# Strassen's scheme a second time, over two pairs of batches, in a fused attention and token-mixing kernel

## The chip, the cores and the metric

The kernel runs on one core of one Trainium2 chip. The metric is the device time of one execution in microseconds (us). A core has five engines that run side by side, each through its own instructions in order: TensorE (PE in the profile; its weight loads are PEld), VectorE (DVE), ScalarE (ACT), GpSimd (POOL) and SyncE (SP). PE writes its results to PSUM; the working memory SBUF has 128 partitions. DMAs are issued from queues: here SP loads inputs and stores results, and POOL issues DMAs that add their data to what stands at the target ("accumulating DMAs").

## What is computed

Four batches, four heads, 1088 positions, 32 features per head; float32 arithmetic to float32 accuracy.

```python
phi(x)  = outer product of S1 x and S2 x           # 8 * 8 features
kv, z   = sum over positions of phi(k) v, of phi(k)
x       = (phi(q) kv) / (phi(q) z + 1e-6)          # (4, 1088, 128): heads side by side
theta   = x @ w_theta
zr, zi  = x * cos(theta), x * sin(theta)
y       = w_tok_r @ zr + w_tok_i @ zi              # over the 1088 positions, for each batch
u       = x + y
out     = u + max(u @ w_ch, 0)
```

The two token-mixing matrices (1088 x 1088, in float64, unpacked to float32 by the kernel) make up most of the matmul work.

## The kernel before

**One order written out by hand.** The kernel first collects all its work as numbered operations: `op(engine, duration, function, writes, reads)` at lines 146 to 198. `SEQUENCE` (line 46) is a list of the 1024 numbers, and `issue` (line 206) issues the operations in that order; each engine executes its own in that order. `PLACES` gives each buffer its slot in a class of buffers (lines 277 to 286): `big` for rows of the matrices and for x, `zs` for z and raw rows, `hf`, `g3`, `g1`, `sm` for smaller things, `ps` for the eight PSUM banks.

**Attention, batch by batch.** Sums over k squared give the scale of a rounding of k to a coarse level `kb` (line 651) and a rest `r = k - kb` (line 656, VectorE). For batches 1 to 3 the product of rest and (k + level) is needed: k is loaded from memory a second time to `kh` (line 649) and the level is added to it by an accumulating DMA (line 658, through `join`, line 323). Chains of small operations (`chain`, line 777) follow, then `levels`, `den`, `numerators` and `theta_stage` (lines 968 to 1133) for each batch: PE, ACT and DVE take turns, with a cosine and a sine on ACT (lines 1048, 1050). Their result is `zt[b]`, the weights for token mixing: real chunks 0 to 7, imaginary chunks 8 to 15, and the 64 last positions of both in one tail chunk.

**Rows.** `weight` (line 581) brings the 17 rows of the matrices in: one load of 1088 KB each, two or three ACT operations, a shift on DVE and an integer addition, on DVE (line 601) or, for rows in `ROWS_ADD`, by an accumulating DMA (line 599).

**Token mixing.** Each matrix is cut at output position 544, which gives four quarters `a11` (real, first half), `a12` (imaginary, first), `a21`, `a22` (second half; line 1216). For a pair of batches (p, q), [[a11, a12], [a21, a22]] times the real and imaginary z of both is a 2 x 2 block product and is made by seven products instead of eight, in the manner of Strassen. A product (`product`, line 1239) is eight chunks of 128 positions into 544 columns, in two PSUM banks of 288 and 256 columns: 16 matmuls. The sums of z that it needs are made on DVE (`zsum`, `ztwo`), the sums of quarters (`asum`, line 1228) in place by eight accumulating DMAs ("D") or on DVE ("V"). `add` (line 1256) adds a product to x; batch q is held scaled by a power of two against p (`balance`, line 1146; `even[5]` takes it back). `finish` (line 1269) makes two or three output parts of a half: the channel matmul, its rectified sum on DVE, a transpose on DVE and four stores, or for parts of 128 columns a form without transpose and one store. `ends` adds the tail chunk.

Pairs are (0, 1) and (2, 3). Product 1 and 2 of a pair need only batch p (`early_products`, line 1302); product 1 is saved to SBUF and added to three places by accumulating DMAs (`carried`, line 1324). `pair_a` (7, 6, 4) and `pair_a_late` (5, 3) belong to the first pair, `pair_b` (6, 4, 7, 5, 3) to the second. PE runs products of the first pair between the theta stages of batches 2 and 3.

Of the kernel before, what the change touches and what calls it, by code (L numbers as in the profile page):

```python
# [37 lines left out]
KDMA = (False, True, True, True)  # L38
RDMA = (False,) * 4
QDMA = (False,) * 4  # L40
ROWS_ADD = (3, 5, 7, 9, 10, 11, 12, 13, 14, 15, 16)
SUMS = {"30": "D", "20": "D", "10": "V", "40": "D", "32": "V"}
CARRY = {(0, 1): "dma", (2, 3): "dma"}
# [203 lines left out]
def kernel(  # L247
# [1144 lines left out]
    def pair_b(pair):  # L1392
# [24 lines left out]
        for j in BOTH:  # L1417
            ends(s5, q, 1, (j,))
# [94 lines left out]
```

## Time and profile before

| | |
|---|---|
| time, three runs | 229.39 us median (228.37 to 229.68) |
| the profiled execution, its own time | 229.23 us |
| its span in the profile | 227.4 us |
| granted PE clock, mean | 0.992 |
| DMA from SP's queue | 30.30 MB, 39.0% of the 16 engines' span |
| DMA from POOL's queue | 16.26 MB, 37.3% |

Busy times are shares of the span. A matmul of float32 leaves two weight loads and two matmul records in the trace. A line number is that of the helper that recorded an operation: 331 for a matmul, 311 and 318 for VectorE's two-input operations, 325 for an accumulating DMA; so the tiles tell more than the line (`ps<-big,zs` is a token-mixing matmul: rows and z into PSUM).

### The profile page before, as it was taken

To read this page: it belongs to the slowest core of one execution; us is meant where nothing else is said; L and a number is where in the kernel's file an instruction comes from. 1 tells how busy PE (TensorE), PEld (TensorE's weight loads), DVE (VectorE), ACT (ScalarE), POOL (GpSimd) and SP (SyncE) were. 2 spreads that over 40 slices of the span, in tenths; PEclk is the share of its full clock that TensorE was granted. 3 is DMA by queue.
4 is the path that set the end of the run, shared out by engine and by line. 5 is a ranking of instruction groups with operands and counts; after the bars stand their busy time and mean duration, and the time that the engine had idled before them with its cause. 6 is when DMAs were issued, how large, how long until landed. Compare 5 with 4: busy or idle time off the path is not lost.

```text
span 227.4 us, 4055 instructions
## 1 busy us (share of the span) xinstructions
PE 217.8 (96%) x1486; PEld 182.2 (80%) x1486; DVE 171.0 (75%) x388; ACT 126.1 (55%) x260; POOL 55.2 (24%) x92
## 2 busy tenths in 40 slices
PE   7999999998979999899989999999999999999993
PEld 3898999976867886588868788888888888888882
DVE  2799999999999989789997917985483663504763
ACT  2988798999999997999997545730000000000000
POOL 1067960001116300013322361968000000000000
PEclk9999999999979999999999999999999999999999
DMA  4999999994999999299999899999973000331442
GB/s 130 421 420 312 383 353 417 419 425 147 246 299 188 299 257 273 89 291 242 275 243 207 255 191 167 176 191 194 198 128 52 0 0 3 62 58 23 69 74 58
DMA packets 28888, 46.80 MB, mean 206 GB/s; under 512 B 18757, under 2 KB 19013, under 8 KB 26693
## 3 DMA queue, kind: packets, MB, share of 16 engines
q1 hardware_dynamic: 22532, 30.30, 39.0%
q0 software_dynamic: 6336, 16.26, 37.3%
q8 instruction: 11, 0.18, 0.3%
q14 instruction: 9, 0.07, 0.1%
HBM read 28.07 MB, written 2.23 MB: 133 GB/s over the span
## 4 chain that ended last, share of the span: by engine, by line
PE 54%; DVE 24%; DMA 10%; ACT 7%; issue 3%; POOL 0%; SPq 0%; DVEq 0%; ACTq 0%; POOLq 0%
PE ps L331 49%; DMA big<-big 5%; DVE big L311 5%; DMA zs<-w_tok 4%; DVE g L311 3%; DVE sm L318 2%; PE ps L366 2%; DVE hf L315 2%; DVE big L315 2%; DVE sm L311 2%; ACT big L591 2%; PE ps L1035 1%; DVE sm L315 1%; DVE lv L311 1%; PE ps L1087 1%
## 5 line engine op out<-in xcount | busy, mean ns | idle before, releaser
L331 PE MATMUL ps<-big,zs 128*128 128x288 f32 (+2 forms) x498 | 116.2, 387 | 2.2 <-DVE zs L311 1.4
L331 PEld LDWEIGHTS ps<-big,zs 128*128 128x128 f32 x498 | 91.2, 191 | 20.5 <-DVE zs L311 1.5
L325 POOL DMA_DIRECT2D big<-big x35 | 33.5, 1347 | 89.9 <-DVE big L315 29.7
L591 ACT ACTIVATE big<-zs 128x544 f32<-128x544 f32 (+1 forms) x33 | 23.3, 727 | 0.7 <-DMA zs<-w_tok 0.7
L594 ACT ACTIVATE big<-zs 128x1088 int32<-128x1088 uint32 (+1 forms) x18 | 21.4, 1190 | 3.1 <-DMA big<-big 1.7
L318 DVE SCALAR_TENSOR_TENSOR big<-ps,even,big 128x288 f32<-128x288 f32 (+2 forms) x23 | 10.5, 483 | 16.1 <-PE ps L331 15.8
L331 PE MATMUL ps<-mf,big 128*128 128x96 f32 x72 | 14.5, 295 | 0.1
L311 DVE TENSOR_TENSOR zs<-ps,g 128x768 f32<-128x768 f32 (+2 forms) x20 | 12.5, 630 | 2.1 <-ACT g L1050 1.7
L315 DVE TENSOR_SCALAR big<-big 128x1088 int32<-128x1088 int32 x17 | 12.2, 725 | 1.3 <-ACT big L591 1.1
L331 PEld LDWEIGHTS <-hf 128*128 128x128 f16 (+1 forms) x144 | 11.9, 105 | 1.2 <-issue 0.8
L311 DVE TENSOR_TENSOR big<-big,ps 128x288 f32<-128x288 f32 (+1 forms) x12 | 5.1, 433 | 9.9 <-PE ps L331 9.8
L311 DVE TENSOR_TENSOR g<-lv 128x768 f32<-128x768 f32 x12 | 11.2, 952 | 1.4 <-PE ps L1087 1.2
L331 PE MATMUL ps<-w,big 128*128 128x128 f32 (+1 forms) x76 | 12.2, 299 | 0.0
L331 PEld LDWEIGHTS ps<-w,big 128*128 128x128 f32 x76 | 10.7, 202 | 1.8 <-PE ps L331 0.6
L318 DVE SCALAR_TENSOR_TENSOR big<-ps,big 128x288 f32<-128x288 f32 (+1 forms) x15 | 6.5, 434 | 6.6 <-PE ps L331 6.5
L331 PEld LDWEIGHTS ps<-mf,big 128*128 128x128 f32 x72 | 10.9, 191 | 0.4 <-issue 0.4
L311 DVE TENSOR_TENSOR big<-big,hf 128x1152 f32<-128x1152 f32 x8 | 11.0, 1385 | 0.0
L325 POOL DMA_DIRECT2D big<-hf x9 | 10.3, 1300 | 2.8 <-DVE sm L315 2.0
L331 PE MATMUL ps<-mv,hf 128*128 128x96 f16 x108 | 10.8, 206 | 0.1
L331 PE MATMUL ps<-big,big 128*128 128x128 f32 x72 | 10.9, 279 | 0.0
L331 PE MATMUL ps<-sbk,g 128*128 128x64 f32 x72 | 9.5, 272 | 0.0
L331 PEld LDWEIGHTS ps<-big,big 128*128 128x128 f32 x72 | 9.3, 192 | 0.1
(195 smaller groups left out, 381.0 us busy)
## 6 DMA issues: line engine op xcount, KB each, us to landing
zs<-w_tok SPq DMA_DIRECT2D x17, 1088.0 KB, 9.6
big<-big POOLq DMA_DIRECT2D x24, 272.0 KB, 8.7
big<-big POOLq DMA_DIRECT2D x11, 544.0 KB, 9.1
big<-k_l SPq DMA_DIRECT2D x7, 576.0 KB, 7.6
big<-q_l SPq DMA_DIRECT2D x4, 576.0 KB, 6.6
big<-v_l SPq DMA_DIRECT2D x4, 576.0 KB, 9.1
big<-hf POOLq DMA_DIRECT2D x3, 576.0 KB, 10.1
big<-hf POOLq DMA_DIRECT2D x6, 272.0 KB, 10.9
```

The costliest lines, as they stand in the source:

```text
L311: eng.tensor_tensor(out=o, in0=a, in1=b, op=f)
L315: (eng or V).tensor_scalar(out=o, in0=a, scalar1=s1, scalar2=s2, op0=op0, **kw)
L318: (eng or V).scalar_tensor_tensor(out=o, in0=a, scalar=s, in1=b, op0=op0, op1=op1)
L325: op("G", n * 2.55e-3, lambda: G.dma_start(dst(), src(), accum_op=ALU.add), w, r, kind=2)
L331: T.matmul(o, lhs, rhs, start=start, stop=stop, skip_group_check=True)
L366: T.matmul(nowhere() if out is None else out, idle()[:, 0:P], idle(), start=True, stop=True, skip_group_check=True)
L591: op("A", 0.19 + (c1 - c0) * 0.0009, lambda c0=c0, c1=c1, scale=scale, alpha=alpha: A.activation(dfn()[:, c0:c1], words_of(raw(), n)[1][:, ...
L594: op("A", 0.22 + n * 0.0009, lambda: A.activation(stp(), words_of(raw(), n)[0].bitcast(U32), AF.Copy, scale=2.0**-29), [stp], [raw])
L1035: T.transpose(x()[:, i], xs()[:, off + i * P:off + (i + 1) * P], ident())
L1087: T.transpose(tr()[:, i * P:(i + 1) * P], qp()[:, i * H + 2 * n:i * H + 2 * n + 2].rearrange("p h i j -> p (h i j)"), ident())
```

## The change

Products 4, 5 and 3 of both pairs use the same quarter (a22, a11, a12) with the z of two pairs. `joint` makes each of them for both pairs at once as a 2 x 2 block product: the quarter is cut into two halves of its chunks and two halves of 272 columns, the two z into their halves of chunks, and seven block products of four chunks and 272 columns take the place of eight (Winograd's form). The sums of blocks of the quarter are `blocks`: two of four on GpSimd, two on VectorE, four operations of 272 columns each; the sums of z are four operations of 512 columns on VectorE. Two of the block products are copied to SBUF by ACT and added to x by accumulating DMAs (`spill`), the others by VectorE (`land`).

So that the batches of both pairs can be used together, batch 2 too is now balanced against batch 0, which puts three scalings on ACT and a ratio on VectorE ahead of its theta stage. The rest goes with it or stands by itself: products 1, 6 and 7 are collected in SBUF (`keep`, `more`) and spread from there by accumulating DMAs; the sum for a11 becomes a negation on ACT and an accumulating DMA ("N"); k plus level is made on VectorE from the k that is there (`KDMA` "V"), without the second load; rows 1, 2, 4, 6 and 8 join `ROWS_ADD`; the sine that loads ACT's table is the first thing on ACT; several small operations are grouped; `SEQUENCE` (968 numbers), `PLACES` and `FILLS` are new.

```diff
-KDMA = (False, True, True, True)
+KDMA = (False, 'V', 'V', 'V')
-ROWS_ADD = (3, 5, 7, 9, 10, 11, 12, 13, 14, 15, 16)
-SUMS = {"30": "D", "20": "D", "10": "V", "40": "D", "32": "V"}
-CARRY = {(0, 1): "dma", (2, 3): "dma"}
+ROWS_ADD = (3, 5, 6, 7, 8, 9, 10, 11, 12, 13, 14, 15, 16, 2, 4, 1)
+SUMS = {"30": "D", "20": "D", "10": "N", "40": "D", "32": "V"}
+JOINT = ("4", "5", "3")
+BLOCKS = {"4": "GGVV", "5": "GGVV", "3": "GGVV"}
+QT = 272
...
+        if eng == "A":
+            pred.update(self.leader)
+            self.leader = self.leader or [o.i]
...
-    op("V", 1.5, constants, [hm, bdm, halfpi, ups, ones, grids], [])
-    op("A", 0.3, lambda: A.activation(warm(), halfpi(), AF.Sin), [warm], [halfpi])
+    op("V", 0.1, lambda: V.memset(halfpi(), math.pi / 2.0), [halfpi], [])
+    op("V", 1.5, constants, [hm, bdm, ups, ones, grids], [])
+    op("A", 1.5, lambda: A.activation(warm(), halfpi(), AF.Sin), [warm], [halfpi])
...
-        if KDMA[b]:
+        if KDMA[b] and KDMA[b] != "V":
             at("loadh", b)
...
-        if KDMA[b]:
+        if KDMA[b] == "V":
+            vop(n, lambda: tt(V, flat(kh()), kc(), flat(kb()), ALU.add), [kh], [kx, kb], lk=1)
+        elif KDMA[b]:
             join(n, lambda: flat(kh()), lambda: flat(kb()), [kh], [kb])
...
-            ts(e[:, 0:2], e[:, 0:2], TINY * TINY, ALU.max, 1.0 / (TINY * TINY), ALU.min)
+            ts(e[:, 0:2], squares()[:, 0:b + 1:b], TINY * TINY, ALU.max, 1.0 / (TINY * TINY), ALU.min)
...
-            if how == "D":
+            if how == "N":
+                op("A", act(HT), lambda i=i: A.mul(dst.ap(i), dst.ap(i), -1.0), [dst.key(i)], [])
+            if how in "DN":
                 join(HT, lambda i=i: dst.ap(i), lambda i=i: y.ap(i), [dst.key(i)], [y.key(i)])
...
+    def keep(name, to):
+        u = buf("hf", (HT,), F32, name)
+        at("acc", name)
+        for j, (c0, c1) in enumerate(PARTS):
+            op("A", act(c1 - c0), lambda j=j, c0=c0, c1=c1: A.copy(u()[:, c0:c1], to.out(j)), [(u, j)], [to.parts[j]])
+        return u
+
+    def more(name, u, to):
+        at("acc", name)
+        for j, (c0, c1) in enumerate(PARTS):
+            vop(c1 - c0, lambda j=j, c0=c0, c1=c1: tt(V, u()[:, c0:c1], u()[:, c0:c1], to.out(j), ALU.add), [(u, j)],
+                [to.parts[j]])
+
+    def spread(b, h, u, c0=0, n=HT, w=None):
+        at("carry", b, "_", h)
+        y = w or u
+        if b and not w:
+            y = buf("hf", (n,), F32, "uq")
+            op("A", act(n), lambda: A.mul(y(), u(), evens[b]()[:, 5:6]), [y], [u, evens[b]])
+        c0 += h * HT
+        join(n, lambda: xT[b]()[:, c0:c0 + n], lambda: y()[:, :n], cells(xT[b], c0, c0 + n), [y])
...
+    def joint(n, a, im, mine, targets, cls, last=False):
...
+        X1, X2 = fresh(x1), fresh(x2)
+        E, F = slab("s" + n, cls)
+        how = BLOCKS[n]
+
+        def zs(k_, d, x, y):
+            at("zj", n, k_)
+            vop(NB * P, lambda: tt(V, d[1](), x[1](), y[1](), ALU.subtract), d[2](), x[2]() + y[2](), lk=1)
+
+        def blocks(k_, d, x, y, f):
+            at("aj", n, k_)
+            eng = how[k_]
+            for i in range(NB):
+                op(eng, pool_(QT) if eng == "G" else dve(QT), lambda i=i: tt(
+                    G if eng == "G" else V, d[0](i), x[0](i), y[0](i), f), [d[1](i)], [x[1](i), y[1](i)], lk=1)
+
+        lo, hi = (0, QT), (QT, HT)
+
+        def sub(k_, to, z, x, cuts=None):
+            at("j", n, k_)
+            for c0, c1 in cuts or [(0, QT)]:
+                to.add((0,), NB * ((c1 - c0) * 4 / 2400 + 0.005), [lambda j, i=i, c0=c0, c1=c1: (
+                    to.out(0)[:, c0:c1], z[0](i), x[0](i)[:, c0:c1]) for i in range(NB)],
+                    z[2]() + [x[1](i) for i in range(NB)])
+            to.close()
...
+        zs(1, X1, z2t, z0t)
+        blocks(0, E, tr, br, ALU.add)
+        zs(2, X2, z2b, X1)
+        blocks(1, F, E, tl, ALU.subtract)
+        zs(3, z2t, z2b, z2t)
+        blocks(2, tr, tl, tr, ALU.subtract)
+        Z, Y, W = [Sum(f"j{n}{c}", (lo,)) for c in "ZYW"]
+        sub(1, Z, z0t, tl)
+        spill(1, Z, bb0, both, lo)
+        sub(2, Y, z0b, bl)
+        blocks(3, bl, bl, F, ALU.subtract)
+        zs(4, z0b, z0b, X2)
...
+        land("y", Y, bb0, lo)
+        sub(6, Z, X2, F)
+        spill(2, Z, bb2, both, lo)
+        sub(5, W, X1, E)
+        land("w", W, bb2, hi, False)
+        sub(7, Z, z2t, tr)
+        land("z", Z, bb2, hi, False)
+        sub(4, Z, z0b, br)
+        land("q", Z, bb0, hi)
...
+        sub(3, W, z2b, bl)
+        land("v", W, bb2, lo)
+        for b in (bb0, bb2):
+            for h in both:
+                if n != "5" or h:
+                    done(b, h, LAST if last and b == bb2 else PARTS)
...
-            largest(pair, j)
-            theta_stage(b, xT[b] if j == 0 else balance(pair))
+            largest(b)
+            theta_stage(b, balance(b) if b else xT[b])
...
+    (pa, qa), (pb, qb) = PAIRS
+    for n in JOINT:
+        if n == "4":
+            joint("4", a22, 1, (pa, pb), ([(1, True)], (pa, pb)), "g3")
+        elif n == "5":
+            joint("5", a11, 0, (pa, pb), ([(0, False), (1, True)], (qa, qb)), "zs")
+        else:
+            joint("3", a12, 1, (qa, qb), ([(0, True)], (qa, qb)), "g3", True)
```

More of the change, by code (lines that the diff above doesn't have):

```diff
@@ L1158, in ratio @@
             stt(e[:, 5:6], e[:, 1:2], 0.5, e[:, 2:3], ALU.mult, ALU.mult)
[L1160 removed]
+        op("V", 1.0, ratio, [even], [(squares, 0), (squares, b)], lk=6)
         return even
@@ L1237, in asum, with product @@
                    [x.key(i), y.key(i)], lk=1)
-    def product(name, to, zz, aa, joint=True, tail=None):
+    def product(name, to, zz, aa, joint=True, tail=None, step=2):
         each = tuple(range(len(to.cuts)))
@@ L1254, in ends, with add @@
             [(zt[b], NG), (rows[NK - 1], h)])
-    def add(name, pair, b, h, to):
-        even = evens[pair]
-        for j, cut in enumerate(to.cuts):
+    def add(name, b, h, to, cuts=None):
+        for j, cut in enumerate(cuts or to.cuts):
             at("acc", name, "_", j)
@@ L1348, in ztwo, with zneg, parts_of, product4 @@
                                                         ALU.subtract), [dst[1](g)], [x[1](g), y[1](g)], lk=1)
+    def zneg(name, dst, x, y):
+        at("zc", name)
+        for g in range(NG):
+            c0, c1 = g * GC, min(g * GC + GC, NF)
+            vop((c1 - c0) * P, lambda c0=c0, c1=c1: stt(dst[0](c0, c1), x[0](c0, c1), -1.0, y[0](c0, c1), ALU.mult,
+                                                        ALU.subtract), [dst[1](g)], [x[1](g), y[1](g)], lk=1)
+    def parts_of(pair):
+        p, q = pair
+        return part(zt[p], 0), part(zt[p], 1), part(zt[q], 0), part(zt[q], 1)
+    def product4(pair):
+        p, q = pair
+        s4 = Sum(f"p4{p}")
+        product(f"4{p}", s4, part(zt[p], 1), a22, tail=(p, 1))
+        add(f"4{p}", p, 1, s4)
+        done(p, 1)
+    def product5(pair, joint):
+        p, q = pair
+        x = str(p)
+        s5 = Sum("p5" + x)
+        product("5" + x, s5, part(zt[p], 0), a11, joint)
+        add("5" + x, q, 0, s5)
+        at("m", "e" + x)
+        for js in [BOTH] if joint else [(j,) for j in BOTH]:
+            ends(s5, q, 1, js)
+        s5.close()
+        add("5" + x + "h", q, 1, s5)
+        done(q, 1)
+    def product3(pair, cuts):
+        p, q = pair
+        s3 = Sum(f"p3{p}", cuts)
+        product(f"3{p}", s3, part(zt[q], 1), a12, cuts is PARTS, tail=(q, 0))
+        add(f"3{p}", q, 0, s3)
+        done(q, 0, cuts)
     def pair_a(pair):
@@ L1375, in pair_a_late @@
         x = str(p)
[L1376 to L1377 removed]
+        how = SUMS["1" + x]
+        asum("1" + x, a11, *((a11, a21, ALU.add) if how == "N" else (a21, a11, ALU.subtract)), how)
         asum("4" + x, a12, a12, a21, ALU.add, SUMS["4" + x])
[L1379 to L1390 removed]
+        if "5" not in JOINT:
+            product5(pair, True)
+        if "3" not in JOINT:
+            product3(pair, PARTS)
     def pair_b(pair):
@@ L1403, in pair_b @@
+        zneg("2" + x, t2, re_p, im_q)
+        s6 = Sum("p6" + x)
+        product("6" + x, s6, t2, a21)
+        more("6" + x, u, s6)
+        spread(q, 0, u)
         asum("3" + x, a21, a21, a22, ALU.subtract, SUMS["3" + x])
         ztwo("4" + x, im_p, im_p, t2)
-        s4 = Sum("p4" + x)
-        product("4" + x, s4, im_p, a22, tail=(p, 1))
-        add("4" + x, pair, p, 1, s4)
+        if "4" not in JOINT:
+            product4(pair)
         zsum("3" + x, re_q, im_q, re_q, ALU.subtract)
-        product("7" + x, sx, re_q, a21)
@@ L1410, in pair_b @@
-        add("7" + x, pair, p, 1, sx)
-        done(p, 1)
-        add("7" + x + "h", pair, q, 1, sx)
-        s5 = Sum("p5" + x)
-        product("5" + x, s5, re_p, a11, joint=False)
-        add("5" + x, pair, q, 0, s5)
-        at("m", "e" + x)
-        for j in BOTH:
-            ends(s5, q, 1, (j,))
-        s5.close()
-        add("5" + x + "h", pair, q, 1, s5)
-        done(q, 1)
-        s3 = Sum("p3" + x, LAST)
-        product("3" + x, s3, im_q, a12, joint=False, tail=(q, 0))
-        add("3" + x, pair, q, 0, s3)
@@ L1425, in pair_b, with slab @@
-        done(q, 0, LAST)
+        s7 = Sum("p7" + x)
+        product("7" + x, s7, re_q, a21)
+        more("7" + x, u, s7)
+        spread(p, 1, u)
+        spread(q, 1, u)
+        if "5" not in JOINT:
+            product5(pair, False)
+        if "3" not in JOINT:
+            product3(pair, LAST)
+    NB = NF // 2
+    def slab(name, cls):
+        if cls == "zs":
+            e = buf("zs", (2, NB, QT), F32, name)
+            return [((lambda i, n=n: e()[:, n, i]), (lambda i, n=n: (e, (n, i)))) for n in range(2)]
+        r = []
+        for n in range(2):
+            e = [buf("g3", (2, QT), F32, f"{name}{n}") for _ in range(NB // 2)]
+            r.append(((lambda i, e=e: e[i // 2]()[:, i % 2]), (lambda i, e=e: (e[i // 2], i % 2))))
+        return r
```

220 lines of the change are left out of this document (111 added, 109 removed), and 126 rows, old and new, of tables (PLACES, SEQUENCE).

## The prediction

> **What bounds the kernel now.** First the page's busy times, then the table of windows, then the chain of waits in order of time.
>
> ```profile
> PE 217.8 (96%) x1486; PEld 182.2 (80%) x1486; DVE 171.0 (75%) x388; ACT 126.1 (55%) x260; POOL 55.2 (24%) x92
> ```
>
> ```profile
> core 0: us, PE busy (x) PEld busy (x) DVE busy (x) ACT busy (x) POOL busy (x), PEclk, DMA share, GB/s
> 150.00:220.00 70.00, 70.00 (x316) 58.16 (x314) 37.87 (x82) 0.00 (x0) 6.98 (x8) 1.00 0.45 77
> 100.00:147.50 47.50, 46.70 (x302) 38.51 (x299) 38.73 (x77) 35.97 (x66) 17.70 (x21) 1.00 1.00 221
> ```
>
> ```profile
> 100.00:110.00 10.00, 10.00 (x70) 8.47 (x67) 9.73 (x19) 9.86 (x19) 3.49 (x4) 1.00 1.04 240
> ...
> 180.00:190.00 10.00, 10.00 (x45) 8.29 (x44) 4.72 (x9) 0.00 (x0) 0.00 (x0) 1.00 0.00 0
> ```
>
> ```profile
> 7.20 0.29 DVE sm L419
> ...
> 56.79 0.27 DVE mv L311
> ...
> 61.13 1.28 ACT L1048
> ...
> 119.52 3.93 PE ps L331 x16
> ...
> 147.55 73.31 PE ps L331 x328
> 220.88 0.47 DVE big L318
> ```
>
> Two regimes are to be seen. Up to some 105 us the attention part sets the pace: the chain is DVE from 7 to 57 us, then ACT (with a table load of 1.28 us on it), DVE and DMA in turn, and between 100 and 110 DVE, ACT and DMA are all at 97% or more. From there PE is bound by itself: it is without work for 0.8 us of 47.5 and then for nothing in 70, at the full granted clock, and the chain ends with 73.3 us of token-mixing products in one piece. In that piece DVE is busy 37.9 of 70 us, ACT not at all, POOL 7. So a product saved is worth its full time on PE, and DVE has 32 us to lend, if what it adds comes in time.
>
> **The saved matmuls.** Between 180 and 190 us PE does nothing but products of this kind: 44 weight loads in 10 us, two for each fp32 matmul, so 0.4545 us for a matmul of about 272 columns. The six products that become joint (products 4, 5 and 3 of both pairs) are 6 x 8 x 2 = 96 such matmuls now and 3 x 7 x 4 = 84 afterwards; the tails stay 12. 12 x 0.4545 = **5.4 us less**, all on the path, since the joint products come where PE is dense. Counted through the new sequence (968 steps), none is issued on PE before the last theta matmul; so PE gives up the products of the first pair that fill it today before 147 us, and fills with products 1, 2, 7 and 6 of both pairs instead. Those are enough: the last theta matmul stands behind the same amount of PE work as before.
>
> **The front.**
>
> ```profile
> L311 DVE TENSOR_TENSOR big<-big,hf 128x1152 f32<-128x1152 f32 x8 | 11.0, 1385 | 0.0
> ...
> L311 DVE CUSTOM_DVE_ANT_0 big<-big,big 128x2176 uint16<-128x2176 uint16 x6 | 7.7, 1284 | 0.1
> ...
> L1027 ACT ACTIVATE g<-big,even 128x384 f32<-128x384 f32 x6 | 3.6, 608 | 1.3 <-DVE even L318 1.3
> ```
>
> k plus level on VectorE adds three operations like the first row, 3 x 1.385 = 4.2 us, in the stretch up to 57 us where DVE is the chain; three k loads and three accumulating DMAs go. Five of the six row additions on DVE become DMAs (5 x 1.284 = 6.4 us less), but only one or two of them stand before 57 us. The sine table is now loaded first, while the inputs are on their way, which takes the 1.28 us off the chain at 61. Batch 2 is now balanced against batch 0: three scalings on ACT (3 x 0.608 = 1.8 us) and a ratio of six small DVE operations. By 57 us this is 4.2 - 1.3 = 2.9 us late, by 105 us DVE is 6.4 - 4.2 - about 1 = 1 us ahead and ACT 1.8 - 1.3 = 0.5 us behind. I take **0**: PE is only bound from 105 us on, where the two have about met. The bounds are +2.9 us (the early delay is never made up) and -3.5 us (6.4 - 4.2 + 1.3, all of it on the chain).
>
> **DVE and POOL beside the joint products.**
>
> ```profile
> L311 DVE TENSOR_TENSOR big<-big,big 128x544 f32<-128x544 f32 x8 | 5.4, 708 | 0.5 <-PE ps L331 0.5
> ...
> L311 DVE TENSOR_TENSOR zs<-ps,g 128x512 f32<-128x512 f32 x4 | 2.7, 687 | 0.0
> ...
> L311 DVE TENSOR_TENSOR big<-big,ps 128x288 f32<-128x288 f32 x6 | 2.7, 451 | 9.8 <-PE ps L331 9.8
> ```
>
> The new work on DVE is 12 sums of z blocks of 512 columns (0.687 us by the nearest row, 8.2 us) and 24 block sums of rows of 272 (0.451 us or less, 10.8 us). The additions of results into x come out level, 30 against 31. The eight subtractions for a11 (8 x 0.708 = 5.7 us) leave DVE, for eight negations on ACT, which is idle there, and eight accumulating DMAs. So DVE has 37.9 + 19 = 57 of some 65 us: covered, with little room, and in order.
>
> POOL gets the other 24 block sums, which it has never done in this trace, and its queue also holds the accumulating DMAs.
>
> ```profile
> L311 POOL TENSOR_TENSOR pbd<-psc,hm 128x128 f32<-128x128 f32 x2 | 1.4, 681 | 1.1 <-DVE psc L315 1.0
> ...
> L311 POOL TENSOR_TENSOR sbt<-sq,hm 128x32 f32<-128x32 f32 x2 | 0.4, 228 | 0.0
> ...
> L311 POOL TENSOR_TENSOR sbk<-s,hm 128x64 f32<-128x64 f32 x1 | 0.3, 293 | 0.1
> ```
>
> ```profile
> 26.56 2.78 POOL L531 COPY mf<-mf 128x64 f32<-128x64 f32 x1
> ...
> 70.91 0.55 POOL L531 COPY mf<-mf 128x64 f32<-128x64 f32 x1
> ...
> 141.09 7.07 POOL L325 DMA_DIRECT2D big<-big  x8 [4.66 <-PE ps L331]
> ```
>
> ```profile
> 26.41 2.85 DVE L311 TENSOR_TENSOR big<-big,hf 128x1152 f32<-128x1152 f32 x2
> ```
>
> From 32 to 64 columns a two-input operation of POOL grows by 65 ns, 2 ns a column: 0.71 us for 272, the lower bound. The row of 128 columns scaled by 272/128 gives 1.45 us, the upper one. The same copy took 0.55 us once and 2.78 us where two DVE operations with both inputs in SBUF ran beside it, just as long as those two; DVE was not slowed (1.39 us each against 1.385). So the loser there was POOL, and DVE's block sums, row sums and z sums are of that very kind. I take 1.0 us, between the bounds and nearer the rows of few columns. The first place that is tight is product 4: between its first and its second block product PE has 24 matmuls, 10.9 us, and POOL six DMA issues of 0.88 us (7.07 / 8) and five block sums, the last of which the second block product reads. It decides at (10.9 - 5.3) / 5 = 1.1 us a sum. At 1.0 us it just holds; for the uneven waits of both engines I put **+0.8 us**, between 0 and the +4.8 us of the first rival.
>
> The Trainium skill (SBUF — State Buffer, Who interferes with whom) speaks against the change here: a VectorE instruction with two SBUF inputs and a GpSimd instruction that reads SBUF exclude one another, and whichever starts second waits for the whole of the first. The copy of 2.78 us agrees; by this rule the sum moves towards the first slower rival below. Its GPSIMD Engine Reference (Elementwise — side-by-side cycle accounting) gives 2.6 cycles per element at 1.2 GHz, an estimate of 0.59 us for 272 columns, by which the 0.8 us would be 0 and the sum 227.0.
>
> **The end.** The sequence now ends with the last block product of product 3, one addition, and the two output parts (288 and 256 columns) of batch 1; today it ends with two parts of 128 columns, stored by one DMA each.
>
> ```profile
> 219.52 0.52 DVE L318 SCALAR_TENSOR_TENSOR big<-ps,even,big 128x288 f32<-128x288 f32 x1 [0.89 <-PE ps L331]
> ...
> 220.68 1.95 PE L331 MATMUL ps<-big,zs 128*128 128x128 f32 x16
> 220.88 0.46 DVE L318 SCALAR_TENSOR_TENSOR big<-ps,big 128x288 f32<-128x288 f32 x1 [0.84 <-PE ps L331]
> 221.38 0.48 DVE L1287 STREAM_TRANSPOSE g<-big 128x288 f32<-128x288 f32 x1
> ```
>
> ```profile
> L1291 SPq DMA_DIRECT2D out<-g x60: 315/451/1056, 170.5 to 223.2; - x60
> ...
> DMA to landing us min/median/max: 1.5/1.7/2.8
> ```
>
> Today the last product ends at 222.63 and the span at 227.4, 4.8 us later. Afterwards: addition 0.52, the wait for the output matmul 0.84, rectifying and transpose 0.46 + 0.48, so 2.35 us to the first store; the second part's four stores queue behind four of the first, eight issues of 0.45 us, the last begun 3.15 us later; 1.7 us to land, and the 0.8 us that lie today between the last landing and the end: 8.0 us. **+3.2 us**. The lower bound is 0 (the other parts are done earlier and nothing queues), the upper +3.6.
>
> **The sum.** The profiled execution's own time is 229.2 us (span 227.4), 0.2 below the median of 229.4. 229.2 - 5.4 + 3.2 + 0 + 0.8 = **227.8 us**, 0.7% below the median. About 0.5%, 1.1 us, is what a measurement here can tell from no change: faster is below 228.2, slower above 230.5.
>
> **Rivals.** *The front gains* (0.14): the row additions and the table load come off the chain entirely and POOL keeps up. For it: DVE at 97% and DMA at 1.04 between 100 and 110, so whatever leaves DVE shows. Against it: 4.2 us of the new work sits at the very start. 229.2 - 5.4 + 3.2 - 3.5 = 223.5 us.
>
> *POOL's block sums are late* (0.22, slower): one mechanism, POOL held up by DVE, at the second block product of 4 and the places like it in 5 and 3. At 1.45 us a sum POOL needs 5.3 + 7.25 = 12.6 us in the first place against 10.9, +1.7; from there to the place in product 5 that reads POOL's first sums it has six issues and nine sums, 18.4 us, against 33 matmuls and three output matmuls on PE, 16.3 us, +2.1; a third of about 1 us in product 3. 229.2 - 5.4 + 3.2 + 4.8 = 231.8 us. It decides from 1.1 us a sum. For it: the 2.78 us; against it: 0.55 us for the same copy.
>
> *The early delay stays* (0.20, slower): the 2.9 us of k sums push every later step, since ACT and DMA behind them are full as well and cannot catch up. 229.2 - 5.4 + 3.2 + 2.9 + 0.8 = 230.7 us.
>
> *The products save nothing* because the block products wait for one another's sums: this needs over 5.4 us of such waits and is held within the first slower rival.
>
> **Chances.** The forecast has 0.44: 0.34 of it faster, 0.10 within 0.5%. Of the late sums 0.20 are slower, 0.02 within; of the early delay 0.18 slower, 0.02 within; the front's gain is faster. Together 0.48 faster, 0.14 the same, 0.38 slower. The forecast's own range is 226 to 229.5. The range for 8 in 10 goes from the front's gain, 223.5, to both slower cases in part, 233.5 (231.8 + about half of 2.9).
>
> **What would show it.** 84 instead of 96 wide matmuls, and still 44 loads in 10 us. The start of the dense stretch and PE's idle time before the second block products show the front and POOL; the duration of POOL's 272-column sums decides between 0.71 and 1.45. The end: some 8 us between the last block product and the end of the span. The prediction is wrong if PE has over 2 us of waits after the theta stages, or if the dense stretch begins over 2 us earlier or later for the same work.

## The result, and the profile after

| | before | changed |
|---|---|---|
| time, us, median (range), 4 runs each | 229.5 (228.4 to 229.7) | 239.2 (238.8 to 240.9) |
| ratio, 95% interval | | 1.046 (1.040 to 1.053) |
| profiled execution: its own time, span | 229.2, 227.4 | 240.9, 238.9 |
| end of the last theta matmul | 147.55 | 151.53 |
| from there to the end of the span | 79.9 | 87.4 |

The change costs 4.6% by the ratio, 4.2% by these medians; 227.8 us was predicted, and 223.5 to 233.5 as the range. In the experiments below, runs over 1.5% above the fastest of their kernel are left out of times and ratios, so the kernel with all sums on VectorE has 232.5 us there, and in the expectations 234.5, the median of all its runs. The last two rows divide the 11.5 us of span: in this execution 4.0 are lost in the front (the part up to the last theta matmul), 7.5 in the late part behind it. For the late part the sum had forecast 79.9 - 5.4 + 3.2 + 0.8 = 78.5 us; 8.9 more were needed. The table of windows, first of before and then of the changed kernel, cut at the last theta matmul (columns: window, its length, then busy time and count for each engine, granted clock of PE, DMA share, GB/s):

```profile
0.00:147.50 147.50, 141.49 (x1139) 119.21 (x1140) 127.82 (x294) 124.06 (x256) 45.76 (x82) 0.99 0.93 274
147.50:227.40 79.90, 76.27 (x349) 63.02 (x347) 43.17 (x95) 2.08 (x6) 9.48 (x11) 1.00 0.46 80
```

```profile
0.00:151.50 151.50, 141.01 (x1143) 118.10 (x1144) 126.59 (x293) 124.91 (x265) 54.92 (x88) 1.00 0.98 272
151.50:238.90 87.40, 73.76 (x307) 59.03 (x305) 68.31 (x127) 9.42 (x17) 41.92 (x46) 0.94 0.58 93
...
167.10:172.00 4.90, 0.03 (x1) 0.03 (x1) 4.80 (x7) 0.00 (x0) 4.82 (x6) 0.81 0.77 133
172.00:177.00 5.00, 5.00 (x11) 3.84 (x12) 4.96 (x8) 0.00 (x0) 2.48 (x3) 0.50 0.55 95
177.00:187.00 10.00, 10.00 (x45) 8.20 (x45) 4.16 (x11) 2.51 (x4) 4.01 (x6) 1.00 0.33 52
...
230.50:238.90 8.40, 1.18 (x4) 0.68 (x4) 2.19 (x5) 0.00 (x0) 0.00 (x0) 0.77 0.33 58
```

PE works 76.3 us in the late part before and 73.8 after, and half of the five microseconds from 172 to 177 is only a clock of 0.50: 11 matmul records there, 45 in the ten at full clock behind. Without that it is 71.3, so 5.0 us of PE work are gone, 0.4 less than the 5.4 of the step on the matmuls. But PE stands still from 167.1 to 172, works at half speed to 177, and waits once more:

```profile
164.64 2.00 PE L336 MATMUL ps<-g,hf 128*128 128x272 f32 x8
...
171.97 4.90 PE L336 MATMUL ps<-big,zs 128*128 128x288 f32 x10 [4.91 <-DVE big L316]
...
192.17 2.07 PE L336 MATMUL ps<-zs,hf 128*128 128x272 f32 x8 [1.37 <-DVE hf L316]
```

4.9 us of waiting, 2.5 us (half of five) of slow clock and 1.4 us of waiting are 8.8 us, where the sum had put 0.8. These 8.0 us more, 0.4 of the matmuls and 0.4 of the end (below) make 8.8 of the 8.9 us. Both waits are for VectorE. What it did in the stretch before, in order of time:

```profile
165.00 1.23 DVE L316 TENSOR_TENSOR hf<-hf,hf 128x544 f32<-128x544 f32 x1
166.15 2.46 DVE L316 TENSOR_TENSOR big<-big,big 128x544 f32<-128x544 f32 x2
...
169.81 2.11 DVE L316 TENSOR_TENSOR big<-big,big 128x544 f32<-128x544 f32 x2
```

The matmuls at 171.97 are product 7 of the second pair; they read the row sums a21 - a22, the 128x544 instructions with two SBUF inputs. VectorE has no gap, and each of these takes 1.1 to 1.3 us. The groups of the changed kernel by shape (count, busy us, mean ns), with POOL's block sums:

```profile
L316 POOL TENSOR_TENSOR g<-big,big 128x272 f32<-128x272 f32 x8 | 13.4, 1671 | 0.0
...
L316 POOL TENSOR_TENSOR g<-g,big 128x272 f32<-128x272 f32 x8 | 10.8, 1359 | 0.2
...
L316 DVE TENSOR_TENSOR big<-big,big 128x544 f32<-128x544 f32 x8 | 9.0, 1148 | 0.0
...
L316 POOL TENSOR_TENSOR zs<-big,big 128x272 f32<-128x272 f32 x4 | 6.3, 1665 | 0.0
...
L316 POOL TENSOR_TENSOR zs<-zs,big 128x272 f32<-128x272 f32 x4 | 4.9, 1214 | 0.2
```

The row sums took 708 ns before and take 1148 now. The spans of POOL's 24 sums add up to 35.4 us, 1.47 each, but they overlap with the spans of the DMA issues beside them, so this is not what a sum costs POOL. In the late part POOL is busy 41.9 us, and 20.2 in the version below that has no sums on it: some 0.9 us a sum. The six issues and five sums ahead of the second block product, for which the prediction made its bounds, run from the first of these two rows to the end of the second:

```profile
152.80 1.75 POOL L330 DMA_DIRECT2D big<-big  x2 [4.08 <-ACT big L1243]
...
160.83 2.27 POOL L316 TENSOR_TENSOR g<-big,big 128x272 f32<-128x272 f32 x1
```

They took 10.3 us (152.80 to 163.10), which is what the prediction has at its 1.0 us a sum, and the block product (the 128x272 matmuls at 164.64, which read POOL's sums of block E) ran without a wait.

The end:

```profile
228.04 2.46 PE L336 MATMUL ps<-big,zs 128*128 128x272 f32 x10
...
232.88 3.80 SPq L1304 DMA_DIRECT2D out<-g  x8
```

The last product ends at 230.50, its eight stores leave SP's queue from 232.88 on, in 3.80 us, and the span ends 8.4 us behind the product; 8.0 were predicted.

### The profile page after: what moved, and what is told of

Same layout as the page of the kernel before. It is cut to its first block, busy times and chain, and to the rows that moved or that the text cites. A ratio compares the mean times of both kernels' runs of the same rounds, so it can differ in the third digit from the quotient of the medians.

```text
span 238.9 us, 4122 instructions
## 1 busy us (share of the span) xinstructions
PE 214.8 (90%) x1448; PEld 177.1 (74%) x1448; DVE 194.9 (82%) x419; ACT 134.3 (56%) x281; POOL 96.8 (41%) x134
## 3 DMA queue, kind: packets, MB, share of 16 engines
HBM read 26.30 MB, written 2.23 MB: 119 GB/s over the span
## 4 chain that ended last, share of the span: by engine, by line
PE 33%; DVE 17%; ACT 15%; issue 12%; DMA 12%; POOL 7%; SPq 0%; POOLq 0%; DVEq 0%; ACTq 0%
PE ps L336 30%; DMA big<-big 8%; POOL big L330 5%; DVE big L316 5%; DMA zs<-w_tok 4%; ACT big L599 3%; DVE g L316 2%; PE ps L370 2%; ACT big L596 2%; POOL g L316 2%; DVE zs L316 1%; DVE hf L320 1%; DVE lv L316 1%; ACT g L1056 1%; DVE sm L320 1%
## 5 line engine op out<-in xcount | busy, mean ns | idle before, releaser
L336 PE MATMUL ps<-big,zs 128*128 128x256 f32 (+2 forms) x408 | 101.6, 401 | 4.9 <-DVE big L316 4.9
L336 PEld LDWEIGHTS ps<-big,zs 128*128 128x128 f32 x408 | 77.3, 193 | 23.8 <-DVE big L316 5.3
L330 POOL DMA_DIRECT2D big<-big x48 | 45.5, 1466 | 87.9 <-DVE big L320 35.6
L1333 ACT ACTIVATE hf<-hf,even 128x544 f32<-128x544 f32 x5 | 3.6, 745 | 27.2 <-DVE hf L316 27.2
L1516 ACT ACTIVATE g<-ps,even 128x272 f32<-128x272 f32 x5 | 2.4, 483 | 28.7 <-PE ps L336 28.7
L316 DVE TENSOR_TENSOR big<-big,hf 128x1152 f32<-128x1152 f32 x11 | 15.0, 1360 | 0.1
L330 POOL DMA_DIRECT2D big<-g x8 | 9.1, 1176 | 14.6 <-ACT g L1516 11.7
L323 DVE SCALAR_TENSOR_TENSOR g<-g,ps 128x384 f32<-128x384 f32 x12 | 6.6, 550 | 9.1 <-ACT g L1052 9.1
L316 POOL TENSOR_TENSOR g<-big,big 128x272 f32<-128x272 f32 x8 | 13.4, 1671 | 0.0
L323 DVE SCALAR_TENSOR_TENSOR big<-ps,even,big 128x272 f32<-128x272 f32 (+2 forms) x23 | 11.1, 489 | 2.2 <-PE ps L336 1.9
```

The source lines that it names most:

```text
L316: eng.tensor_tensor(out=o, in0=a, in1=b, op=f)
L323: (eng or V).scalar_tensor_tensor(out=o, in0=a, scalar=s, in1=b, op0=op0, op1=op1)
L330: op("G", n * 2.55e-3, lambda: G.dma_start(dst(), src(), accum_op=ALU.add), w, r, kind=2)
L336: T.matmul(o, lhs, rhs, start=start, stop=stop, skip_group_check=True)
L1333: op("A", act(n), lambda: A.mul(y(), u(), evens[b]()[:, 5:6]), [y], [u, evens[b]])
L1516: op("A", act(QT), lambda: A.mul(w(), to.out(0), evens[b]()[:, 5:6]) if b else A.copy(w(), to.out(0)), [w], [to.parts[0]] + ([evens[b]] if ...
```

## The experiments

Every time is a median, and every ratio is to runs of the kernel before on the same chip; "turn" is the end of the last theta matmul in the run's profile, and "late part" the rest of the span.

### Who slows whom

Two versions take POOL's sums away. The first gives them to VectorE, the second puts copies on ScalarE in their place (the additions of the blocks are left out):

```diff
-BLOCKS = {"4": "GGVV", "5": "GGVV", "3": "GGVV"}
+BLOCKS = {"4": "VVVV", "5": "VVVV", "3": "VVVV"}     # first
+BLOCKS = {"4": "AAVV", "5": "AAVV", "3": "AAVV"}     # second, "A": A.copy(d[0](i), x[0](i))
```

> Changed kernel with the 24 block sums that POOL makes moved to VectorE (nothing else). Changed kernel: 239.2 us, TensorE idle 4.91 us at 167 us behind VectorE's row sums, those 128x544 sums 1.148 us each (0.708 before), granted clock 0.50 for some 6 us behind it. Theory 'shared way' (POOL's sums and VectorE's sums with both inputs in SBUF hold each other up): the 128x544 sums fall back to 0.70 to 0.75 us; VectorE gets 24 x 0.43 = 10.4 us of work, some 4 us of it ahead of the wait, against 6 us that its slowed instructions give back there: wait 1 to 3 us, no half clock, 233 to 236 us. Rival 'POOL's queue' (the block sums hold up the accumulating DMAs queued behind them): wait gone, but the 128x544 sums stay above 1 us; 231 to 234 us. Rival 'VectorE has too much work': the wait grows to 8 us or more, 241 to 244 us.

> Changed kernel with the 24 block sums of POOL replaced by copies of their first input on ScalarE: the additions of the blocks E and F are left out, order and number of instructions stay. Theory 'shared way': 128x544 sums at 0.70 to 0.75 us, the 4.9 us wait at 167 us and the half clock behind it are gone: 230 to 233 us. Rival 'POOL's queue': wait gone too, but the 128x544 sums stay near 1.15 us. Rival 'VectorE has too much work': wait and half clock stay, 238 to 240 us.

Measured: 232.5 us, 1.013 (1.007 to 1.020), with the sums on VectorE; 229.4 us, 0.999 (0.995 to 1.002), with the copies (their profiled execution took 232.0; its turn came at 152.2, and only its late part is used here). Groups and late part of the first, then of the second:

```profile
L316 DVE TENSOR_TENSOR big<-big,big 128x544 f32<-128x544 f32 x8 | 5.6, 715 | 0.2 <-PE ps L336 0.2
...
L316 DVE TENSOR_TENSOR g<-big,big 128x272 f32<-128x272 f32 x8 | 3.5, 432 | 0.0
```

```profile
166.19 0.72 PE L336 MATMUL ps<-g,hf 128*128 128x272 f32 x2 [2.23 <-DVE g L316]
```

```profile
152.20:230.20 78.00, 70.66 (x307) 57.65 (x305) 55.74 (x127) 17.30 (x40) 20.22 (x23) 0.97 0.66 106
160.00:170.00 10.00, 10.00 (x45) 8.30 (x45) 8.49 (x17) 4.20 (x10) 3.25 (x4) 1.00 1.10 186
170.00:180.00 10.00, 10.00 (x45) 8.24 (x44) 5.72 (x13) 3.27 (x7) 1.73 (x3) 1.00 0.60 100
```

The row sums are back at 715 and 722 ns. The wait of 4.9 us ahead of product 7 is gone in both. The first has another in its place, 2.2 us ahead of the block product that reads the sums of block E, which VectorE now makes itself; the second has none, and its clock is full from 160 to 180. Its late part is 78.0 us, with the same 127 instructions on VectorE as the changed kernel's, which take 55.7 us in place of 68.3. So sums on POOL cost VectorE 12.6 us in its own instructions. "VectorE has too much work" falls: with 24 more sums on it, the wait ahead of product 7 goes.

The same by itself, one execution of a kernel that does none of the reference's work, only such instructions, alone and side by side:

> A kernel of its own, with none of the reference's work: VectorE and POOL instructions alone and beside each other. Alone: VectorE's 128x544 sum of two SBUF inputs 0.71 us, POOL's 128x272 sum unknown (0.76 us was its fastest in the changed kernel). Theory 'shared way': together both grow, VectorE's to 1.1 to 1.5 us and POOL's to 1.3 to 1.8 us; VectorE with one input in PSUM (128x272, 0.49 us) and VectorE with one input in all (128x1088, 0.72 us) stay within 5% beside POOL. Rival (POOL's sums are slow by themselves, VectorE's by the DMA traffic): both stay as they are alone.

Windows of that kernel (the counts are instructions; a few at the edges are tiny ones that bring the engines together):

```profile
43.20:50.90 7.70, 0.00 (x0) 0.00 (x0) 7.70 (x14) 0.00 (x0) 0.00 (x0) 0.50 0.00 0
51.20:59.80 8.60, 0.00 (x0) 0.00 (x0) 0.31 (x2) 0.00 (x0) 8.60 (x14) 0.50 0.00 1
60.00:73.80 13.80, 0.00 (x0) 0.00 (x0) 13.80 (x13) 0.00 (x0) 13.80 (x12) 0.50 0.00 0
79.90:85.60 5.70, 0.00 (x0) 0.00 (x0) 5.33 (x14) 0.00 (x0) 0.00 (x0) 0.50 0.24 98
86.00:94.50 8.50, 0.00 (x0) 0.00 (x0) 7.92 (x19) 0.00 (x0) 8.50 (x12) 0.50 0.00 0
97.80:106.90 9.10, 0.00 (x0) 0.00 (x0) 8.72 (x14) 0.00 (x0) 0.00 (x0) 0.50 0.00 0
107.30:121.10 13.80, 0.00 (x0) 0.00 (x0) 13.41 (x13) 0.00 (x0) 13.80 (x12) 0.50 0.00 0
```

VectorE alone needs 7.7 us for twelve 128x544 sums (0.64 each), POOL alone 8.6 us for twelve of 128x272 (0.72). Together POOL's twelve need 13.8 us, 1.15 each, and VectorE gets some 11 done in that time, 1.2 each: both lose. With one input in PSUM (fifth row against the fourth) POOL needs 8.5 us, as alone, and VectorE 0.47 an instruction, as alone. The fourth part of the expectation was wrong: a 128x1088 multiplication by a constant has one SBUF input and still slows POOL to 13.8 us and itself from 0.76 to some 1.2. The Trainium skill (SBUF — State Buffer, Who interferes with whom) has both cases: two SBUF inputs, or a form that works in the two-port mode, as such multiplications can, share POOL's way; one SBUF input in another mode does not. Its "fully blocks (not throttle)", taken for the whole of both instructions, would by estimate make a pair 0.64 + 0.72 = 1.36 us; 1.15 was measured, so a part of each ran beside the other.

Then the other way around, POOL sums put into the kernel before:

```diff
 op(how, ..., lambda: tt(E, dst.ap(i), x.ap(i), y.ap(i), f), ...)
+tt(G, idle()[:, 0:272], dst.ap(i)[:, c:c + 272], w2...[:, 0:272], ALU.add)    # same step, once or twice
```

> Kernel before with 24 sums of 128x272 added on POOL (first input the row that VectorE has just summed, second a constant; the result is used by nothing): one behind each of the eight row sums a11 - a21, two behind each of the eight a21 - a22. Nothing else is changed. Theory 'shared way': the second row sums, 0.708 us each before, take 1.0 to 1.3 us; POOL's sums 1.1 us or more. Whether the time follows depends on TensorE's lead there: 229 to 232 us. Rival (a kernel's DMA traffic and not POOL slowed them in the changed kernel): the row sums stay below 0.8 us.

Measured: 238.2 us, 1.038 (1.034 to 1.043), and the row sums that the theory named did not grow:

```profile
L311 DVE TENSOR_TENSOR big<-big 128x544 f32<-128x544 f32 x8 | 6.7, 852 | 8.4 <-DMA big<-big 8.4
...
L311 DVE TENSOR_TENSOR big<-big,big 128x544 f32<-128x544 f32 x8 | 5.5, 715 | 5.7 <-DMA big<-big 5.3 <-PE ps L331 0.5
```

The second row sums keep 715 ns (708 before); the first go from 720 to 852. This is no case against the shared way: an added sum reads the row that VectorE has just made, and beside the second row sums POOL always starts behind VectorE. Beside the first ones both orders occur:

```profile
150.06 0.76 POOL L311 TENSOR_TENSOR idle<-big,w 128x272 bf16<-128x272 f32 x1 [3.69 <-DVE big L311]
150.19 1.21 DVE L311 TENSOR_TENSOR big<-big 128x544 f32<-128x544 f32 x1
151.33 0.71 DVE L311 TENSOR_TENSOR big<-big 128x544 f32<-128x544 f32 x1
151.55 1.11 POOL L311 TENSOR_TENSOR idle<-big,w 128x272 bf16<-128x272 f32 x1 [0.73 <-DVE big L311]
```

In both pairs the one that starts first takes as long as alone, and the second waits for it: VectorE 1.21 us in the first pair, POOL 1.11 in the other. But the 9 us go another way:

```profile
142.46 3.90 PE L331 MATMUL ps<-big,zs 128*128 128x288 f32 x16 [2.10 <-DMA big<-big]
...
165.00 10.18 PE L331 MATMUL ps<-big,zs 128*128 128x288 f32 x36 [3.82 <-DVE zs L311]
```

The added sums wait in POOL's queue for the rows of VectorE, and the accumulating DMAs queue behind them. PE waits for two of these DMAs (2.1 us, and 1.4 at 196 us) and 3.8 us for a z sum, which stands on VectorE behind a row sum that waited 4.9 us for such a DMA (1.0 before). That the queue is the way is read from this trace and was not tried by itself. So sums in POOL's queue can cost as much through the queue as through the shared way. In the changed kernel itself the runs above put the loss on the shared way: there, row sums with POOL's sums beside them took 1.148 us, and 0.72 without.

### The halved clock

```diff
+if name == "72" and not i and not j:
+    for _ in range(14): spin(to.parts[0]())     # idle matmuls ahead of product 7, second pair
```

> Changed kernel with 14 idle matmuls (0.32 us each by the profile of before) on TensorE in front of product 7 of the second pair, where it waits 4.91 us and then runs at a granted clock of 0.50 for some 6 us. Theory 'idle time halves the clock': TensorE stays busy there, the clock of the slices behind stays 1.00, the ten matmuls that took 4.90 us take 2.5 us, and the time falls by 2.5 to 3.5 us to 235.5 to 237 us. Rival (the clock falls by another cause): the slices stay at 0.50, 239 us or more.

Measured: 237.1 us, late part 84.9 in place of 87.4.

```profile
170.95 2.56 PE L336 MATMUL ps<-big,zs 128*128 128x288 f32 x10 [2.64 <-DVE big L316]
```

```profile
173.60:180.00 6.40, 6.40 (x29) 5.30 (x28) 3.55 (x8) 0.75 (x1) 3.05 (x5) 1.00 0.26 44
```

The idle matmuls run, PE still waits 2.6 us, and then has the full clock: the ten matmuls take 2.56 us in place of 4.90. Product 7 starts as late behind the turn as before (20.4 us), so the 2.5 us are the halved clock, and it went when part of the idle time was filled.

### The tail

Three tries. Exchange which output is finished last, and finish it in 0:256, 256:416 and 416:544; all sums on VectorE and every second of the last stores issued by ScalarE; all sums on VectorE and the last output in four parts, three of them with a single store:

```diff
-done(b, h, LAST if last and b == bb2 else PARTS)
+done(b, h, ENDS if last and b == bb0 else PARTS)             # first; ENDS as above
+(A if (b, h) == (1, 0) and f % 2 else SY).dma_start(...)     # second
+done(b, h, (ENDS if b == bb0 else LAST) if last else PARTS)  # third; ENDS 0:160:288:416:544
```

> Changed kernel with the finishing of the two last outputs exchanged: the batch whose product ends last is finished in the columns 0:256 (ahead of that product), 256:416 and 416:544, the other one in two parts. Theory 'tail' (what follows the last product is its finishing and eight stores, 8.4 us): five stores are left behind the last product, the tail falls to 5 to 6.5 us, the time by 2 to 3.4 us to 236 to 237.5 us. Rival (the stores share a rate and the other batch's come late instead): tail and time as they were within 0.5 us, 239 us.

> The kernel with all block sums on VectorE (234.5 us), and in the finishing of the last output every second store issued from ScalarE's DMA queue. There eight stores leave SP's queue one after the other in 3.80 us, and the tail behind the last product is 8.4 us. Theory 'the issues of one queue set the tail': the last issue 1.5 to 2 us earlier, tail 6.4 to 6.9 us, 232.5 to 233 us. Rival 'the stores' landing sets it': tail 8 us or more, 234 to 235 us.

> All block sums on VectorE (234.5 us), and the last output finished in the columns 0:160 (ahead of the last product), 160:288, 288:416 and 416:544, each of the last three with a single store; the output before it in three parts as the last one was before the change (6 stores in place of 8). Theory 'issues behind the last product set the tail': three stores are left there in place of eight, tail 4.7 to 5.8 us in place of 8.4 us, 231 to 232 us. Rival 'what is queued on SP sets it', as in the exchange of the two outputs: tail 7.5 us or more, 234 us.

Measured: 241.8, 237.0 and 231.4 us (ratios 1.052, 1.037 and 1.009). SP's queue in the first and in the third, and what it waited for in the second:

```profile
204.59 31.45 SPq L1305 DMA_DIRECT2D out<-g  x47
236.13 0.38 SPq L1297 DMA_DIRECT2D out<-g  x1
```

```profile
225.99 1.33 SPq L1298 DMA_DIRECT2D out<-g  x3
```

```profile
SPq L1304 <- DMA out<-g: 4.3, 1, 4.3
```

In the first the rival held for the tail: the eight stores of the other output now stand right before, 47 issues in one row, the last one leaves at 236.13, and the tail is 8.5 us. In the second a store on SP's queue waited 4.3 us for a store to land, and the tail grew to 9.6 us: the rival's side (8 or more), with a time beyond its 234 to 235. In the third three issues are left behind the product (end 223.08): tail 6.5 us in place of 8.4. That is neither the 4.7 to 5.8 expected nor the rival's 7.5; three matmuls of the output still stand between. So what helped is fewer issues on SP's queue, neither another order of them nor a second queue. The time of the third is only 1.1 us below that of the version with eight stores (232.5). In their two profiled executions 1.9 us are won in the tail and 0.4 at the turn, and 1.7 lost again to a halved clock ahead of product 7, of which more at the end.

### The front

Five runs. The old order for the stages up to theta, in the changed kernel; in the kernel before, K on VectorE and all rows by DMA, then K alone; and in the version with the shorter tail, five rows back on VectorE, then K back to a load and an accumulating DMA:

```diff
-KDMA = (False, True, True, True)
+KDMA = (False, 'V', 'V', 'V')
-ROWS_ADD = (3, 5, 7, 9, 10, 11, 12, 13, 14, 15, 16)
+ROWS_ADD = (3, 5, 6, 7, 8, 9, 10, 11, 12, 13, 14, 15, 16, 2, 4, 1)
```

> Changed kernel in which the instructions of the stages up to the theta turns stand in the order that they had before the change (buffers placed anew to fit it); the additions of K on VectorE and of all rows of the weights by DMA stay. Last theta turn on TensorE: 147.55 us before, 151.37 us changed. Theory 'order' (the front lost 3.8 us because the new order lets TensorE wait between 70 and 100 us): turn at 147 to 148.5 us, and 2.5 to 4 us less in all: 235 to 237 us. Rival 'operations' (the additions of K on VectorE or the rows' DMAs cost it): turn at 150.5 us or later, 238 to 240 us.

> Kernel before with two of the changed kernel's edits to its front and nothing else: K plus its levels on VectorE in place of a second load and an accumulating DMA, and the words of all sixteen rows joined by DMA; the order is that of before. Last theta turn on TensorE: 147.55 us before, 149.1 to 152.2 us in the runs of the changed kernel so far. Theory 'operations': the turn falls 2 to 4 us late here too, 231.5 to 234 us. Rival 'order': the turn stays within 1 us of 147.5 us, 228.5 to 230.5 us.

> Kernel before with K plus its levels on VectorE alone (the rows as they were). With both edits in the order of before the time was 251.7 us, with TensorE waiting 7.28 us on an accumulating DMA at 80 us. Theory 'the rows' DMAs did that, K on VectorE costs nothing': 227 to 230 us, turn within 1.5 us of 147.55 us. Rival 'K on VectorE costs as much as it weighs, 3 x 1.3 us or more': 232 us or more.

> As the run with the shorter tail, with the words of rows 1, 2, 4, 6 and 8 joined on VectorE as before the change (1.3 us each) in place of an accumulating DMA; same order. Last theta turn on TensorE: 149.1 to 152.2 us with the DMAs, 147.55 us before the change. Theory 'the rows' DMAs cost the front': turn at 147 to 148.5 us. Rival 'they cost nothing, VectorE is full at 70 to 90 us (9.9 and 9.6 of 10 us)': turn 1 to 5 us later, 152 us or more.

> As the run with the shorter tail, with K plus its levels by a second load and an accumulating DMA, as before the change, for batches 1 to 3. Theory 'the three additions on VectorE (1.3 us each) cost the front': turn 2 to 4 us earlier than 149.1 to 152.2 us. Rival 'the loads cost as much': turn at 150 us or later.

| kernel | time | turn |
|---|---|---|
| old order of the front | 309.6 | 222.9 |
| before, K and rows | 250.7 | 170.9 |
| before, K alone | 233.1 | 150.7 |
| short tail, rows on VectorE | 234.6 | 152.2 |
| short tail, K by DMA | 242.3 | 161.9 |
| short tail (to compare) | 231.4 | 148.8 |

Each edit is slower than the kernel that it was put into, by 3 to 22 us, and the old order with the new operations by far the most (it also places its buffers anew, so it shows little). K on VectorE alone, in the order of before, puts the turn 3.1 us later. The rows' DMAs gain 3.2 us of time in the new order; the turn alone would not show it, since it differs by as much between kernels with the same front (below). K by DMA had its loads placed by hand, so its 13 us at the turn say more of the place than of the operation. A cleaner run takes the operation out and leaves the order: a memset on POOL writes the target of the sum, K plus level is left out.

> As the run with the shorter tail (231.4 us, last theta turn at 148.8 us), with the addition of K and its levels on VectorE left out for batches 1 to 3 (a memset on POOL writes its target instead); same order. Theory 'each of these additions holds up the front, whose VectorE is 94 to 100% busy from 10 to 100 us': turn 2.5 to 4 us earlier, 145 to 146.5 us, time 227.5 to 229 us. Rival 'the order of the front sets it': turn within 1.2 us of 148.8 us, time 230.3 us or more.

Turn 148.9 us against 148.8, time 229.8 against 231.4, with intervals of the ratio that overlap (1.004 to 1.012, 1.007 to 1.012). The 2.5 to 4 us at the turn that the theory asked for are not there, so the additions of K are not what holds the changed front up; a smaller share of theirs is not excluded. In eight kernels that have the changed front as it is, the turn came at 148.8 to 152.2 us, 1.2 to 4.7 later than before. What is seen is PE without work at places where it had some, here in two stretches of the changed kernel and then in the same two of the kernel before:

```profile
70.00:80.00 10.00, 7.93 (x64) 6.14 (x63) 9.90 (x18) 9.58 (x20) 0.00 (x0) 1.00 1.02 278
...
90.00:100.00 10.00, 7.91 (x50) 6.12 (x50) 7.20 (x22) 8.80 (x17) 0.20 (x1) 1.00 0.64 139
```

```profile
70.00:80.00 10.00, 9.88 (x85) 8.42 (x86) 9.76 (x18) 9.78 (x22) 5.83 (x9) 1.00 1.02 255
...
90.00:100.00 10.00, 9.18 (x78) 7.44 (x78) 8.06 (x13) 9.80 (x22) 0.86 (x1) 1.00 0.52 197
```

With the ten between, PE has 4.2 us less work from 70 to 100 us. The waits are for ScalarE and VectorE, each over 7 us busy in every ten, in many pieces of 0.3 to 1.4 us. That the new order as a whole costs this is what is left, and is not shown by a run of its own.

### What is left in the late part

From the version with the shorter tail, which waits 2.2 us for the sums of E at 166 us: eleven block sums that nothing near by needs are moved behind the last row sum of product 7, and two short groups of matmuls ahead of the one that waits. Then five more moves of that kind, three of them in the front.

> As the run with all block sums on VectorE and the shorter tail (231.4 us), where TensorE still waits 2.2 us near 166 us for the sums of block E on VectorE: the eleven block sums on VectorE that nothing near by needs (those of F and of the next products) are moved behind the last row sum of product 7, and two short groups of matmuls that need none of the sums (the product of an output and a tail) are moved ahead of the block product that waits. Theory 'VectorE's queue ahead of the product sets the wait': wait below 0.8 us, 229 to 230 us, the same as the kernel before within 0.5%. Rival 'the wait moves to product 7': a wait of 1.5 us or more there, 231 to 232 us.

> As the late-order run (230.0 us), with five more moves within the same instructions: a group of matmuls ahead of one that waits 0.83 us for VectorE at 136 us, a row's preparation on ScalarE behind the copies that TensorE waits 1.04 us for at 97 us, one copy on ScalarE earlier at 72 us, and on VectorE the difference and the sums of F that the block product at 180 us waits 0.85 us for ahead of other sums. Theory 'what is left are waits of TensorE on queue order': 1.5 to 3 us less, 227 to 228.5 us, at or below the kernel before. Rival 'the waits move on': 229.5 us or more.

Measured: 229.9 us, 1.0035 (1.0004 to 1.0066), and 230.5 us, 1.007 (1.004 to 1.010).

```profile
166.38 0.73 PE L338 MATMUL ps<-g,hf 128*128 128x272 f32 x2 [0.49 <-DVE g L318]
```

The wait is 0.5 us, with 0.9 more at 180, and the late part 78.4 us (span 228.6 less turn 150.2), what the prediction had for it, though with the shorter tail. It is the best version that leaves nothing out, and some 0.35% above the kernel before, not below it. The five further moves gave nothing: the waits at 136 and 180 us went, one of 1.3 us for a DMA came at 108 us.

## Why the prediction was wrong, point by point

- **The saved matmuls, -5.4: right.** PE has 5.0 us less work in the late part, and with copies in place of POOL's sums, and the tail as it was, the late part is 78.0 us, where 79.9 - 5.4 and the 3.6 of the tail make 78.1.
- **DVE and POOL, +0.8: the step that failed most.** Its sentence was "DVE was not slowed ... So the loser there was POOL", read from one copy beside two long VectorE instructions, and from it followed "57 of some 65 us: covered". The work itself was counted well: from the turn on it is 55.7 us without POOL's sums. With them it was 68.3: the runs show both engines as losers, 0.64 to 1.2 us and 0.72 to 1.15 us side by side. PE then waited 4.9 and 1.4 us for VectorE, 6.3 in place of 0.8. The rival "POOL's block sums are late" does not describe this: in its first place POOL kept to 1.0 us a sum, below its condition of 1.1, and PE waited for VectorE's row sums for product 7, not for POOL's sums. That its 231.8 lies nearer the result is luck.
- **The halved clock, not in the sum.** 2.5 us followed the long wait. The row for it stood in the profile of before, where PE's clock was 0.83 between 60 and 70 us.
- **The front, 0: wrong, +4.0** in the profiled execution, beyond its bound of +2.9, and 1.2 to 4.7 in the eight kernels with this front. It was costed as work per engine, and work is not what decides: VectorE has 126.6 us of it up to the turn, 1.2 less than before. The rival "the early delay stays" has the right sign, and in the order of before K on VectorE did cost 3.1 us at the turn; in the new order nothing was seen to come back without it. What in the new order costs the front its time stays open.
- **The end, +3.2: right in mechanism,** 8.4 us in place of 4.8, +3.6, its upper bound.

Put together: 227.8 + 4.0 (front) + 8.8 - 0.8 (waits and clock) + 0.4 (tail) + 0.4 (matmuls) = 240.6 us, against 240.9 of the profiled execution.

## What to carry to other kernels

Work given to POOL beside a busy VectorE is priced by what it takes from both: here 24 sums on POOL cost VectorE 12.6 us, more than the 10.4 us (24 x 0.43) that it needs to make them itself. Ask which instructions have both inputs in SBUF, and who waits for those; of the two other kinds tried, sums with one input in PSUM lost nothing and long multiplications by a constant lost as much. A wait of PE in a dense stretch can cost more than its length (4.9 us cost 7.4 here), and a front full on three engines was not costed by sums of work per engine: operations that came with a new order were worse in the old one, and the other way around.

## What the runs showed of the hardware that was not expected

The clock. In three places PE was without work and then at a clock of 0.50: 4.9 us here, 2.23 us in the run with the shorter tail, and 1.40 us in the kernel before at 63 to 65 us. A window behind the second wait, then three around the third (0.68 and 0.72 us without work, then 0.50):

```profile
168.00:169.00 1.00, 1.00 (x4) 0.76 (x3) 1.00 (x3) 0.00 (x0) 0.00 (x0) 0.50 0.55 96
```

```profile
63.00:64.00 1.00, 0.32 (x3) 0.18 (x2) 1.00 (x2) 0.94 (x5) 0.75 (x1) 1.00 1.03 318
64.00:65.00 1.00, 0.28 (x1) 0.28 (x2) 1.00 (x2) 1.00 (x3) 0.00 (x0) 1.00 1.02 344
...
66.00:67.00 1.00, 1.00 (x5) 0.91 (x4) 0.96 (x2) 1.00 (x3) 0.00 (x0) 0.50 1.04 248
```

A wait of the same 2.23 us in the first run with all sums on VectorE left the clock at 1.00 (its ten matmuls took 2.46 us, in the shorter-tail run 4.14), and so did 2.6 us behind the idle matmuls. The Trainium skill (TensorE: Matmul & The Clock Gate, What's actually happening) gives one idle window of some 3.4 us as the condition; the 4.9 us agree, the 1.40 and the 2.23 do not. Worked out from the clock of windows of one us, the stretch at 0.50 was 3.4 us long behind each of the two short waits and 6.8 us with the long one, where it began some 3.1 us after the last matmul. How the chance depends on the idle time was not tried.
